# Attention and two feed-forward layers on one core: score matmuls of two heads side by side, norms by matmul, and an offset for every kind of task

## The chip, the core and the metric

One core of a Trainium2 chip runs the whole program. The metric is the device time of one execution in microseconds (us); three runs of the kernel before took 1132.02 to 1135.79 us, median 1133.86.

## What is computed

```python
# attention: batch 4, 8 heads, 576 positions, 64 dimensions per head
scores = (q @ k.T) / sqrt(64)
x = log1p(|i - j|) / log1p(max(i, 1))
scores += relu(x * w1 + b1) @ w2          # 32 hidden units, one bias per head
a = softmax(scores) @ v                   # -> 2304 tokens x 512
# first feed-forward layer (512 -> 2048 -> 512), then the second
h = relu(a @ moe_w_in);  y = (s * h*h + b) @ moe_w_out
g = y @ moe2_w_in;       out = (g - tanh(g)) @ moe2_w_out
```

## The kernel before

Every matmul operand is split into a high part in fp16 and a low part (the rest, also fp16), each under one scale that is a power of two; a product is the sum of high x high, high x low and low x high. The scales come from norms, which are computed on the chip first.

**Units.** Attention is cut into 144 units: one head of one batch entry with 128 rows of queries (128 "full" units), or two heads with the last 64 rows (16 "half" units). Batch entries 0 and 1 come first (72 units), then 2 and 3. A unit's work, in `unit_tasks` (line 716):

- `qk` on TensorE (L749): scores into a PSUM tile `sp`. In the array's 128 rows lie 64 dimensions of the keys' high part and 64 of their low part, and the queries stand there twice, so that a unit takes four matmuls of 288 columns (two halves of the 576 keys, the queries' high and low part). A half unit puts its two heads into 64 columns each and takes eight.
- `ttr` on VectorE (L763, L767): adds the bias `bi`, takes the row's maximum.
- `ex` on ScalarE (L773): the exponential into `e`, with the row's sum. `hi` (L782 on VectorE or L784 on ScalarE) copies `e` to fp16, `lo` (L790, GpSimd) takes the rest, `tr` (L796, a DMA) transposes both into `et`.
- `pv` on TensorE (L809, L816): 14 matmuls with the values into `xp`.

`x_tasks` scales a group of four units, splits it and transposes it into `xt`, the input of the first feed-forward layer. Two `sp` tiles, two `e`, three `hl`, four `et` and one `xp` exist.

**Before the units.** `scan_tasks` loads keys, queries and values of a batch entry and sums their squares on ScalarE (L591); `part_sum` (L423) adds over partitions, `qk_scales` makes the scales. `k_tasks` makes high and low part of two heads' keys in four steps of 64 partitions each (L359/L357 for the high part, L362 for the low), `q_tasks` those of a group's queries, after a DMA from `qd`, where the queries stand twice. `bias_tasks` makes the biases of 16 rows for all heads, 36 times: hidden units (L454, L458 or L462), 8 matmuls (L466, tile `pb`), a copy to `et` and a DMA to DRAM. `norm_in_tasks`, `w1_conv`, `w1_split` prepare the weights of the first layer (L918 to L924, L974, L362); `cols_out` (L1134, tile `pcs`) sums columns of its second matrix once all of that is split, and `out_done` (L1028, `bcol`) follows.

**The feed-forward layers.** The first runs in nine blocks of 256 tokens, each as soon as its units are done: 192 matmuls `ph` (L1221), relu and square on ScalarE, high part on VectorE, low part on GpSimd, 192 matmuls `po` (L1289). When all units are done (`turn`) the weights of the second layer are loaded and split where the attention's tiles were. Its matmuls are `pg` (L1517) and `pq` (L1564).

**The order.** Nothing is ordered by hand. Every step is a task with a list of engines and costs, tasks that it needs, buffers that it takes, and a due time `prio`. `Schedule.forward` plays the program with these costs: again and again it takes the engine that can start first, and on it, among the tasks that can start within `EPS` of that, the one due first. The order in which it does so is the order of the instructions on each engine, fixed in the program. `tau(u)` gives the due time of unit u; bias, keys, queries and blocks hang on it by constants (lines 26 to 31).

## Time and profile before

| | us |
|---|---|
| median of three runs (lowest, highest) | 1133.86 (1132.02, 1135.79) |
| profiled execution: time | 1135.39 |
| profiled execution: span | 1133.6 |
| TensorE matmul busy | 1026.7 |
| VectorE busy | 786.0 |
| ScalarE busy | 569.0 |
| GpSimd busy | 344.5 |

The span runs from the first to the last instruction; 1.8 us of the execution lie around it. Busy times are sums over an engine's instructions. Matmuls are pipelined and their ends are modelled, so what one matmul really takes is read from the distance of starts, not from its own duration. The granted clock is the share of TensorE's full 2.4 GHz that the chip let through.

### The profile page before, as it was taken

The page shows a single profiled execution, that of the slowest core. Times are in us where ns is not written, and L with a number is a line of the kernel's source. Part 1 is how long each engine was busy: PE and PEld are TensorE (multiplying, and loading weights), DVE is VectorE, ACT ScalarE, POOL GpSimd, SP SyncE. Part 2 cuts the span into 40 slices and gives each one's busy share as a digit, 9 for nine tenths or more (in the row PEclk, how much of TensorE's full clock was granted, in tenths as well). Part 3 has the DMA queues.
Part 4 walks back from the last instruction along what each step waited for, and adds up shares of the span by engine and source line. Part 5 has one row for each costly group of instructions (what it writes and reads, how often), then busy time and mean ns, then how long its engine had stood idle before and what let it go on. Part 6 is the DMA issues. An engine that isn't in the chain of part 4 may idle for free.

```text
span 1133.6 us, 23200 instructions
## 1 busy us (share of the span) xinstructions
PE 1026.7 (91%) x9023; PEld 695.8 (61%) x9026; DVE 786.0 (69%) x1642; ACT 569.0 (50%) x1116; POOL 344.5 (30%) x371
## 2 busy tenths in 40 slices
PE   3366787998999989999999999989999999999998
PEld 1132364776787777878888788877554444444443
DVE  6999899988657898786875668898655444354310
ACT  6999887667667585565663444641211111111100
POOL 6043154436545266575764321400000000000000
PEclk9566797899999999999999999999999999999999
DMA  9887885888999989999997453441010000000000
GB/s 336 288 213 213 200 277 118 186 191 203 197 216 244 237 191 182 195 176 191 199 187 129 161 179 126 154 130 43 5 46 10 19 10 10 19 10 15 14 19 28
DMA packets 260701, 157.79 MB, mean 139 GB/s; under 512 B 199408, under 2 KB 226672, under 8 KB 260592
## 3 DMA queue, kind: packets, MB, share of 16 engines
q1 hardware_dynamic: 260592, 156.33, 58.2%
q8 instruction: 70, 1.15, 0.4%
q14 instruction: 39, 0.32, 0.1%
HBM read 89.04 MB, written 20.05 MB: 96 GB/s over the span
## 4 chain that ended last, share of the span: by engine, by line
PE 60%; DVE 20%; DMA 7%; ACT 5%; issue 4%; POOL 2%; SPq 1%; DVEq 0%; ACTq 0%; POOLq 0%
PE pq L1564 16%; PE pg L1517 16%; PE po L1289 10%; PE ph L1221 8%; DMA et<-hl 5%; PE sp L749 3%; PE pb L466 3%; DVE sp L763 2%; PE xp L809 2%; DVE ks L362 1%; PE xp L816 1%; DVE w1big L921 1%; ACT e L773 1%; DVE vp L362 1%; DVE hr L1244 1%
## 5 line engine op out<-in xcount | busy, mean ns | idle before, releaser
L790 POOL TENSOR_TENSOR hl<-e,hl 128x64 f16<-128x64 f32 (+1 forms) x288 | 232.2, 829 | 229.9 <-ACT hl L784 82.9
L1289 PE MATMUL po<-hr,w1big 128*128 128x256 f16 x1728 | 204.6, 273 | 6.9 <-ACT x L1308 4.3
L1564 PE MATMUL pq<-w1big,w2big 128*128 128x512 f16 (+1 forms) x960 | 195.3, 358 | 0.0
L1289 PEld LDWEIGHTS <-w1big 128*128 128x128 f16 x1728 | 165.8, 98 | 33.6 <-issue 8.3
L1221 PEld LDWEIGHTS <-w1big 128*128 128x128 f16 x1728 | 166.9, 98 | 31.1 <-issue 10.1
L1525 ACT ACTIVATE t<-pg,ich 128x512 f32<-128x512 f32 (+1 forms) x80 | 51.5, 644 | 245.6 <-PE pg L1517 245.6
L1517 PE MATMUL pg<-hr,w2big 128*128 128x512 f16 x768 | 173.6, 379 | 0.0
L1529 DVE SCALAR_TENSOR_TENSOR t<-pg,ich,t 128x512 f32<-128x512 f32 (+1 forms) x80 | 55.7, 696 | 148.9 <-ACT t L1525 148.9
L1517 PEld LDWEIGHTS <-w2big 128*128 128x128 f16 x960 | 95.0, 99 | 96.7 <-issue 4.7
L1564 PEld LDWEIGHTS <-w2big 128*128 128x128 f16 x960 | 93.9, 98 | 94.0
L773 ACT ACTIVATE e<-sp,mx 128x576 f32<-128x576 f32 x144 | 105.6, 733 | 76.0 <-POOL hl L790 48.6
L1248 POOL TENSOR_TENSOR hr<-r,hr 128x512 f16<-128x512 f32 x72 | 96.6, 1342 | 153.8 <-DVE hr L1244 137.0
L763 DVE CUSTOM_DVE_ANT_0 sp<-sp,bi 128x576 f32<-128x576 f32 x144 | 109.3, 759 | 41.5 <-PE sp L749 21.1
L749 PE MATMUL sp<-ks,qs 128*128 128x288 f16 (+1 forms) x640 | 101.7, 303 | 22.2 <-ACT e L773 20.0
L1221 PE MATMUL ph<-xt_own,w1big 128*128 128x256 f16 x960 | 113.8, 274 | 4.4 <-ACT et L359 2.6
L1221 PE MATMUL ph<-w1big 128*128 128x256 f16 x768 | 88.2, 273 | 0.3 <-DVE na L1180 0.3
L749 PEld LDWEIGHTS <-qs 128*128 128x128 f16 (+1 forms) x640 | 54.3, 104 | 47.6 <-issue 31.8
L809 PEld LDWEIGHTS <-et 128*128 128x128 f16 (+1 forms) x1440 | 57.0, 103 | 28.5 <-issue 13.2
L809 PE MATMUL xp<-vp,et 128*128 128x64 f16 (+1 forms) x1440 | 65.2, 198 | 9.9 <-DMA et<-hl 6.1
L784 ACT ACTIVATE hl<-e 128x576 f16<-128x576 f32 x92 | 62.0, 677 | 16.4 <-DMA et<-hl 15.0
L466 PE MATMUL pb<-hr,cst_sb 128*32 128x288 f32 x268 | 41.2, 589 | 28.4 <-DVE et L357 10.9
L1234 ACT ACTIVATE r<-ph 128x512 f32<-128x512 f32 x72 | 42.6, 591 | 40.2 <-PE ph L1221 38.5
(165 smaller groups left out, 1286.2 us busy)
## 6 DMA issues: line engine op xcount, KB each, us to landing
bi<-btd SPq DMA_DIRECT2D x64, 288.0 KB, 3.7
btd<-et SPq DMA_DIRECT2D x36, 288.0 KB, 4.3
qst<-in_qd SPq DMA_DIRECT2D x36, 256.0 KB, 3.8
w1big<-in_win SPq DMA_DIRECT2D x8, 1024.0 KB, 7.9
w1big<-in_wout SPq DMA_DIRECT2D x8, 1024.0 KB, 6.5
w2raw<-in_win SPq DMA_DIRECT2D x8, 1024.0 KB, 5.5
w2raw<-in_wout SPq DMA_DIRECT2D x8, 1024.0 KB, 4.9
x2d<-x SPq DMA_DIRECT2D x36, 128.0 KB, 3.0
```

The source lines that it names most:

```text
L466: nc.tensor.matmul(out=pb[32 * t:32 * t + 32, 0:HS], lhsT=w2d_sb, rhs=hid_t[Q, t][:, hf * HS:(hf + 1) * HS], start=True, stop=True,)
L749: nc.tensor.matmul(out=s_[r0:r0 + r, hf, 0:HS], lhsT=qs.tile[:, s, c * r:c * r + r], rhs=ks.tile[:, a, hf * HS:(hf + 1) * HS], start=s == ...
L763: nc.vector.tensor_tensor_reduce(out=st, in0=st, in1=bi.tile.rearrange("p (a b) -> p a b", a=2), scale=-1.0 / KAP, scalar=3.0e38, op0=ALU. ...
L773: nc.scalar.activation(out=put(e, row_tile("e")).rearrange("p (a b) -> p a b", a=2), in_=sp.tile[:, :, 0:HS], func=AF.Exp, scale=-1.0, bia ...
L784: nc.scalar.activation(out=h[:, 0:S], in_=e.tile, func=AF.Copy)
L790: nc.gpsimd.tensor_tensor(out=hl.tile[:, o:o + m], in0=e.tile[:, c:c + m], in1=hl.tile[:, c:c + m], op=ALU.subtract)
L809: nc.tensor.matmul(out=xp[r0:r0 + r, col:col + 64], lhsT=et.tile[:, n, r0:r0 + r], rhs=vp.tile[:, 0, n % 5, 64 * a:64 * a + 64], start=n = ...
L1221: nc.tensor.matmul(out=ph.tile[:, fi, :], lhsT=win_ap(1, sw, m, f), rhs=xa(sx, m), start=m == 0 and j == 0, stop=m == KM - 1 and j == 2,)
L1248: nc.gpsimd.tensor_tensor(out=rh[:, :, 1, :], in0=r.tile, in1=rh[:, :, 0, :], op=ALU.subtract)
L1289: nc.tensor.matmul(out=po.tile[:, :NB1], lhsT=wout_ap(1, sw, f, c), rhs=rhl[f // 8][:, f % 8, sr, :], start=f == 0 and j == 0, stop=f == K ...
L1517: nc.tensor.matmul(out=pg.tile[:, :n], lhsT=win_ap(2, sw, m, f), rhs=xh[:, sx, m, :n], start=m == 0 and i == 0, stop=m == KM - 1 and i == 2,)
L1564: nc.tensor.matmul(out=pq.tile[:, :n], lhsT=wout_ap(2, sw, f, c), rhs=g[:, sr, :n], start=f == 0 and i == 0, stop=f == KF - 1 and i == 2,)
```

## The change

1. **Scores (`qk`).** Keys of two heads lie in the array's rows 0 to 63 and 64 to 127, their high and low part in two tiles. The two heads of a pair of full units are done by one task of 12 matmuls of 64 rows each, which alternate between the halves of the array and write into two `sp` tiles; it takes both. A half unit takes 12 as well. The order of units inside a batch entry changes with it (`unit_of`): two heads of a pair follow each other.
2. **Keys and queries.** `k_tasks` has two steps of 128 partitions in place of four of 64. `q_tasks` loads all eight heads of a batch entry and 128 rows once, from `qT`, in place of two loads from `qd`: 20 loads, copies and low parts in place of 36.
3. **First norms.** For batch entries 0 and 1 the squares on ScalarE are replaced by matmuls (tile `gram`, 112 of 128 columns) of the upper 16 bits of each value with themselves, and a maximum over each row on VectorE.
4. **Order.** Costs of the player are changed (GpSimd's bias tile 2.45 for 1.5, `PACE`, `HOP`, `COLD`), due constants too, and a table `SHIFT` adds an offset to the due time of each kind of task, some 500 of them. A ring's check counts all buffers that a task takes.
5. **Transposes of `x`.** The layout of `xt` follows the new order of heads; a half group takes four small transposes in place of two.

```diff
-SHARE0, QP, QA, SCU, QG = 31, 8, 19, 48, 7
-T0, R0, T1, RU = 58.44, 2.06, 98.62, 3.64
+SHARE0, QP, QA, SCU, QG = 21, 8, 19, 15, 7
+T0, R0, T1, RU = 56.98, 2.21, 35.64, 3.33
...
-EPS, COLD = 0.02, 100.0
+EPS, COLD, COLD_PACE = 0.02, 190.0, 1.45
+SHIFT = {
+    ".begin": 7.58, ".fn": -21.6, ".lambda": 12.08, "scan0.fn": -26.47, "scan0.mm": -51.47, "scan0.add": -45.69,
...
-    HOP = 0.2
+    HOP = 0.23
+    PACE = dict(pe=1.0, act=1.02, dve=1.06, pool=1.0)
...
-        t.opts, t.fn, t.prio, t.takes = opts, fn, prio, tuple(takes)
+        t.key = self.tag + "." + fn.__code__.co_name.strip("<>")
+        t.opts, t.fn, t.prio, t.takes = opts, fn, prio + SHIFT.get(t.key, 0.0), tuple(takes)
...
+    def unit_of(u):
+
+        b, it, g, k = units[u]
+        if rows_of[it] < 128:
+            return b, it, k, None, k
+        return b, it, 2 * g + k // 2, k % 2, 2 * (k % 2) + k // 2
...
-                {DVE: 0.45, ACT: 0.67, **({POOL: 1.5} if Q < QG else {})}, lambda e, Q=Q, t=t: hid(Q, t, e), deps, d, [hid_i[Q, t]] if Q >= QA else []
+                {DVE: 0.45, ACT: 0.67, **({POOL: 2.45} if Q < QG else {})}, lambda e, Q=Q, t=t: hid(Q, t, e), deps, d, [hid_i[Q, t]] if Q >= QA else []
...
-            ts = sc.add({ACT: 0.16 + 0.86e-3 * n_}, sq, [tl, t0], prio, [jk] if jk else [], [st] if st else [])
...
+                for c in range(n_ // 128):
+                    x = t[:, c, :, 1]
+                    nc.tensor.matmul(
+                        out=gi.tile[:, int(kq), :], lhsT=x, rhs=x, start=c == 0 and col in (0, 4, 8),
+                        stop=c == n_ // 128 - 1 and col in (1, 5, 10),
+                    )
+            tg = sc.add({PE: 0.07 * n_ / 128 + 0.1}, mm, [tl, gram[1]], prio - 500, [gi] if new else [], [gi])
...
+                    nc.vector.tensor_reduce(out=s3, in_=gi.tile[:, 0:n, :], op=ALU.max, axis=AX.X)
...
-        h0 = sc.add({ACT: 0.79, DVE: 0.46}, lambda e: hi(0, e), deps, due - 4, [ks], us)
-        h1 = sc.add({ACT: 0.79, DVE: 0.46}, lambda e: hi(1, e), deps + [h0], due - 4, [], [ks] + us)
-        l0 = sc.add({DVE: 0.86}, lambda e: lo(0, e), [h0], due - 2, [], [ks] + us)
-        l1 = sc.add({DVE: 0.86}, lambda e: lo(1, e), [h1], due - 2, [], [ks] + us)
+        th = sc.add({ACT: 0.67, DVE: 0.46}, hi, deps, due - 4, [ks], us)
+        tl = sc.add(
+            {DVE: 0.78}, lambda _: low_part(ks.tile[:, 1], src(), sc_t[b]["k"], ks.tile[:, 0]), [th], due - 2, [],
+            [ks] + us,
+        )
...
+        src = qT[b, :, it * 128:it * 128 + r].rearrange("(p k) r -> k p r", k=128)
...
-            s_ = put(sp, ps_s.tile([128, 2, 512], F32, tag="s", name="sp"))
+
             r = rows_of[it]
-            heads = [(0, g, p)] if full else [(0, 0, 2 * p), (64, 1, 2 * p + 1)]
-            for s in range(2):
-                for hf in range(2):
-                    for r0, a, c in heads:
+            to = [s_of[v] for v in ((u - 1, u) if full else (u,))]
+            for i in to:
+                put(i, ps_s.tile([128, 2, 512], F32, tag="s", name="sp"))
+            for hf in range(2):
+                for n, (sq, sk) in enumerate(((0, 0), (0, 1), (1, 0))):
+                    for h in range(2):
+                        half = hf if full or h == 0 else 1 - hf
+                        out = to[h].tile[:, half, 0:HS] if full else to[0].tile[64 * h:64 * h + 64, half, 0:HS]
                         nc.tensor.matmul(
-                            out=s_[r0:r0 + r, hf, 0:HS], lhsT=qs.tile[:, s, c * r:c * r + r],
-                            rhs=ks.tile[:, a, hf * HS:(hf + 1) * HS], start=s == 0, stop=s == 1,
+                            out=out, lhsT=qs.tile[64 * h:64 * h + 64, sq, p * r:p * r + r],
+                            rhs=ks.tile[64 * h:64 * h + 64, sk, half * HS:(half + 1) * HS], start=n == 0, stop=n == 2,
                         )
...
+        if not full or a == 1:
+            two = [s_of[u - 1], sp] if full else [sp]
+            t_qkm[u] = sc.add(
+                {PE: 0.95}, qk, t_klo[b, p] + t_khi[b, p] + [t_qlo[b, it], t_last[0]] + first, d - 1000, two, [ks, qs],
+            )
```

How the order moves is shown at three places. The first is the start of ScalarE, where the norms were (`e,ss` are the squares, `hr` and `xt_own` hidden units of the bias, `et` their evacuation, `ks` the keys' high part). Before:

```order
L462 ACT_TABLE_LOAD
L462 ACTIVATE hr<-u_sb,cst_sb 128x576 x2
L591 ACTIVATE e,ss_124<-w1big 128x1152 x2
L462 ACTIVATE hr<-u_sb,cst_sb 128x576
L359 ACTIVATE et<-pb,cst_sb 128x576
L591 ACTIVATE e,ss_124<-w1big 128x1152
L462 ACTIVATE hr<-u_sb,cst_sb 128x576 x4
L591 ACTIVATE e,ss_124<-w1big 128x1152
L462 ACTIVATE hr<-u_sb,cst_sb 128x576 x2
L359 ACTIVATE ks<-w1big,qkc_303 64x576
```

And the changed kernel there:

```order
L556 ACT_TABLE_LOAD
L556 ACTIVATE hr<-u_sb,cst_sb 128x576 x2
L556 ACTIVATE xt_own<-u_sb,cst_sb 128x576
L444 ACTIVATE et<-pb,cst_sb 128x576
L556 ACTIVATE xt_own<-u_sb,cst_sb 128x576
L556 ACTIVATE hr<-u_sb,cst_sb 128x576 x2
L444 ACTIVATE et<-pb,cst_sb 128x576
L556 ACTIVATE xt_own<-u_sb,cst_sb 128x576
L444 ACTIVATE et<-pb,cst_sb 128x576
L556 ACTIVATE hr<-u_sb,cst_sb 128x576 x3
L444 ACTIVATE ks<-w1big,qkc_314 128x576 x3
```

The squares are gone, bias work has their place, and the keys come as rows of 128 partitions.

The second is VectorE where the first layer's second matrix is ready (`w1big<-w1big,w1o_c` are its last splits, `bcol` follows the column sums; `ISA sp,mx` is a unit's score row). Before:

```order
L362 SCALAR_TENSOR_TENSOR w1big<-w1big,w1o_c 128x1024 x2
L763 ISA sp,mx<-sp,bi 128x2x288
L763 ISA mx 128x1
L767 TENSOR_SCALAR mx<-mx 128x1
L763 ISA sp,mx<-sp,bi 128x2x288
L763 ISA mx 128x1
L767 TENSOR_SCALAR mx<-mx 128x1
L869 CAST xh<-xf 128x256
L870 TENSOR_TENSOR xh<-xf,xh 128x256
L362 SCALAR_TENSOR_TENSOR qs<-qst,qkc_398,qs 128x512
L458 TENSOR_SCALAR hid<-u_sb,cst_sb 128x576 x3
L1028 TENSOR_SCALAR bcol<-pcs,w1o_ic,cst_sb 128x4
```

And the changed kernel there:

```order
L447 SCALAR_TENSOR_TENSOR w1big<-w1big,w1o_c 128x1024
L447 SCALAR_TENSOR_TENSOR qs<-qst,qkc_314,qs 128x512
L1009 CAST xh<-xf 128x256
L1010 TENSOR_TENSOR xh<-xf,xh 128x256
L901 ISA sp,mx<-sp,bi 128x2x288
L901 ISA mx 128x1
L905 TENSOR_SCALAR mx<-mx 128x1
L901 ISA sp,mx<-sp,bi 128x2x288
L901 ISA mx 128x1
L905 TENSOR_SCALAR mx<-mx 128x1
L1388 CAST hr<-r 128x2x256
L1172 TENSOR_SCALAR bcol<-pcs,w1o_ic,cst_sb 128x4
```

Ahead of `bcol` stand 27 score rows before and 30 now. On TensorE, ahead of the column sums, stand 192 bias matmuls, the scores of 27 units and the values of 24 before; 232, 30 and 28 now; and all 192 `ph` of the first block in both.

The third is TensorE at one unit's scores, in batch entries 2 and 3. Before:

```order
L816 MATMUL xp_6577<-vp_6068,et_6569 128x64
L749 LDWEIGHTS qs_6603
L749 MATMUL sp_6717<-ks_5679,qs_6603 128x288
L749 LDWEIGHTS qs_6603
L749 MATMUL sp_6717<-ks_5679,qs_6603 128x288
```

And the changed kernel, the first third of a pair's scores:

```order
L955 MATMUL xp_6930<-vp_5359,et_6828 128x64
L869 LDWEIGHTS qs_6809
L869 MATMUL sp_6950<-ks_5773,qs_6809 128x288
L869 LDWEIGHTS qs_6809
L869 MATMUL sp_6951<-ks_5773,qs_6809 128x288
```

The matmuls now alternate between two score tiles; a pair has twelve, where two units had eight.

## Rows read from the trace of the kernel before

**Rows 1.** The page's busy times and its 40 slices of the span.

```profile
PE 1026.7 (91%) x9023; PEld 695.8 (61%) x9026; DVE 786.0 (69%) x1642; ACT 569.0 (50%) x1116; POOL 344.5 (30%) x371
...
PE   3366787998999989999999999989999999999998
...
DVE  6999899988657898786875668898655444354310
...
PEclk9566797899999999999999999999999999999999
```

**Rows 2.** Busy time of each engine in four stretches.

```profile
core 0: us, PE busy (x) PEld busy (x) DVE busy (x) ACT busy (x) POOL busy (x), PEclk, DMA share, GB/s
0.00:204.00 204.00, 130.52 (x1192) 71.96 (x1196) 184.89 (x340) 171.92 (x295) 78.66 (x73) 0.75 0.81 231
204.00:620.00 416.00, 396.12 (x4760) 324.48 (x4759) 318.60 (x834) 264.59 (x579) 232.10 (x276) 0.99 1.00 198
620.00:770.00 150.00, 140.61 (x1286) 124.18 (x1285) 119.53 (x185) 72.80 (x152) 33.72 (x24) 0.98 0.43 142
770.00:1133.60 363.60, 359.47 (x1791) 175.16 (x1789) 162.95 (x284) 59.70 (x90) 0.00 (x0) 1.00 0.06 19
```

**Rows 3.** Timeline of TensorE at the column sums (start, us, what, idle before).

```profile
198.58 3.57 PE L1134 MATMUL pcs<-onesh,w1big 128*128 128x1 f16 x128
```

**Rows 4.** Timeline of VectorE at the same place.

```profile
195.33 2.97 DVE L362 SCALAR_TENSOR_TENSOR w1big<-w1big,w1o_c 128x1024 f16<-128x1024 f32 x2
...
203.63 0.27 DVE L1028 TENSOR_SCALAR bcol<-pcs,w1o_ic,cst_sb 128x4 f32<-128x4 f32 x1
```

**Rows 5.** Groups by line and shape: count, busy us, mean ns, idle before.

```profile
L362 DVE SCALAR_TENSOR_TENSOR ks<-w1big,qkc,ks 64x576 f16<-64x576 f32 x16 | 13.0, 814 | 0.4
...
L362 DVE SCALAR_TENSOR_TENSOR qs<-qst,qkc,qs 128x512 f16<-128x512 f32 x36 | 32.7, 907 | 0.4
...
L591 ACT ACTIVATE e<-w1big 128x1152 bf16<-128x1152 f32 x8 | 9.2, 1156 | 1.0 <-DMA w1big<-in_kT 0.8 <-DMA w1big<-in_qT 0.2
...
L454 POOL TENSOR_SCALAR hr<-u_sb,cst_sb 128x576 f32<-128x576 f32 x6 | 14.7, 2462 | 5.3 <-DVE u_sb L431 5.3
```

**Rows 6.** Timeline of TensorE, full units at 518 us, half units at 601 us.

```profile
518.00 0.43 PE L809 MATMUL xp<-vp,et 128*128 128x64 f16 x9
518.26 0.41 PE L816 MATMUL xp<-vp,et 128*128 128x64 f16 x5
518.61 0.66 PE L749 MATMUL sp<-ks,qs 128*128 128x288 f16 x4
519.11 1.47 PE L1289 MATMUL po<-hr,w1big 128*128 128x256 f16 x12
520.42 0.65 PE L749 MATMUL sp<-ks,qs 128*128 128x288 f16 x4
...
601.32 0.68 PE L749 MATMUL sp<-ks,qs 128*64 128x288 f16 x8
601.93 1.48 PE L1289 MATMUL po<-hr,w1big 128*128 128x256 f16 x12
```

**Rows 7.** TensorE's bias matmuls at the start: timeline, and the group in 0 to 100 us.

```profile
6.27 1.42 PE L466 MATMUL pb<-hr,cst_sb 128*32 128x288 f32 x4 [6.27 <-DVE hr L458]
...
13.02 1.18 PE L466 MATMUL pb<-hr,cst_sb 128*32 128x288 f32 x16
...
L466 PE MATMUL pb<-hr,cst_sb 128*32 128x288 f32 x176 | 26.5, 575 | 22.0 <-DVE et L357 10.9 <-DVE hr L458 6.3 <-POOL hr L454 4.2
```

**Rows 8.** Timeline of all engines: the unit whose scores start at 518.61.

```profile
519.84 0.76 DVE L763 CUSTOM_DVE_ANT_0 sp<-sp,bi 128x576 f32<-128x576 f32 x1
...
520.69 0.15 DVE L767 TENSOR_SCALAR mx<-mx 128x1 f32<-128x1 f32 x1
...
522.81 0.74 ACT L773 ACTIVATE e<-sp,mx 128x576 f32<-128x576 f32 x1 [1.15 <-POOL hl L790]
523.45 0.19 ACT L773 ACTIVATION_READ_ACCUMULATOR e<-sp,mx 128x1 f32 x1
```

**Rows 9.** The page's group of score matmuls, with what ended the idle time before them.

```profile
L749 PE MATMUL sp<-ks,qs 128*128 128x288 f16 (+1 forms) x640 | 101.7, 303 | 22.2 <-ACT e L773 20.0
```

More of the change, by code (lines that the diff above doesn't have):

```diff
@@ L53 @@
     __slots__ = (
-        "opts", "fn", "deps", "prio", "takes", "eng", "at", "end", "done", "left", "next", "seq",
+        "opts", "fn", "deps", "prio", "takes", "eng", "at", "end", "done", "left", "next", "seq", "key",
     )
+ENGINES = ("pe", "act", "dve", "pool", "sp", "turn")
 class Schedule:
-    HOP = 0.2
+    HOP = 0.23
+    PACE = dict(pe=1.0, act=1.02, dve=1.06, pool=1.0)
     DMA_START, DMA_DONE = 0.65, 2.0
@@ L147, in forward @@
             else:
-                if eng == "pe" and at < COLD:
-                    cost = cost * 1.6
+                cost *= COLD_PACE if eng == "pe" and at < COLD else self.PACE.get(eng, 0.0)
                 free[eng] = t.end = at + cost
@@ L375, in tile_kernel @@
                 groups += [(b, it, g) for g in range(2) for b in pr]
-    units = [g + (p,) for g in groups for p in range(NP)]
+    units = [g + (k,) for g in groups for k in range(NP)]
     NG, NU = len(groups), len(units)
@@ L384, in tau, with units_of @@
         return T0 + R0 * u if u < 16 else T1 + RU * (u - 16)
+    def unit_of(u):
[3 more added lines that the diff above has]
+        return b, it, 2 * g + k // 2, k % 2, 2 * (k % 2) + k // 2
+    def units_of(**kw):
+        for u in range(NU):
+            b, it, p, a, c = unit_of(u)
+            d = dict(b=b, it=it, p=p)
+            if all(d[k] == v for k, v in kw.items()):
+                yield u
     def first_unit(**kw):
-        for u, (b, it, g, p) in enumerate(units):
-            d = dict(b=b, it=it, g=g, p=p)
-            if all(d[k] == v for k, v in kw.items()):
-                return u
+        return next(units_of(**kw))
     def last_unit(**kw):
-        return max(
-            u for u, (b, it, g, p) in enumerate(units) if all(dict(b=b, it=it, g=g, p=p)[k] == v for k, v in kw.items())
-        )
+        return max(units_of(**kw))
     ones16 = const.tile([128, 128], BF16, name="ones16")
@@ new lines, in qk @@
+                            rhs=ks.tile[64 * h:64 * h + 64, sk, half * HS:(half + 1) * HS], start=n == 0, stop=n == 2,
+                        )
+        first = [x for Q in range(QP) for x in t_bmm[Q]] if u < 2 else []
+        if not full or a == 1:
[3 more added lines that the diff above has]
+            )
+            t_last[0] = t_qkm[u]
+            if full:
+                t_qkm[u - 1] = t_qkm[u]
+                unit_rest(u - 1)
+            unit_rest(u)
@@ L758, in unit_tasks, with unit_rest @@
+    s_of, t_last = {}, [None]
+    def unit_rest(u):
+        sc.tag = f"u{u // 4 if u < 40 else 10 + u // 16}"
+        b, it, p, a, col = unit_of(u)
+        n, k = u // NP, u % NP
+        full = rows_of[it] == 128
+        d = tau(u)
+        bi, sp = bi_of[u], s_of[u]
+        e, hl, et = inst("e"), inst("hl"), inst("et")
+        vp, sm_i, xp_i = vp_t[b, p], sum_of[n], xp_of[n]
         mx = {}
```

188 lines of the change are left out of this document (105 added, 83 removed), and 75 rows, old and new, of the table SHIFT.

## Prediction

> **What bounds the kernel now.** I read the page's slices first, then the busy time by stretch, then timelines where the bound changes. In the slices [rows 1] TensorE is starved for the first seven of 40 and its granted clock stays below full speed there, while VectorE is at 8 or 9 tenths; afterwards TensorE is nearly always full. The stretches [rows 2] put numbers on it. Up to 204 us VectorE is busy 184.9 us of 204, ScalarE 171.9, TensorE 130.5 at a granted clock of 0.75. From 204 to 620 TensorE is busy 396.1 of 416 at 0.99 and VectorE 318.6; from 620 to 770 it is 140.6 of 150, and after that 359.5 of 363.6. So there are two laws. Before 204 us VectorE and ScalarE set the pace; after it, what TensorE has still to do sets the end, and work taken from the other engines buys nothing there.
>
> The border is one event. The first layer's second matmuls wait for the column sums, which start at 198.58 [rows 3] right after VectorE's last two splits, from 195.33 on; its first use of the sums is at 203.63 [rows 4]. The question is therefore: when does this event come, and how much TensorE work is left behind it?
>
> **The change, part by part.**
>
> *VectorE up to the event.* The order gives the counts. Eight low parts of keys fewer (0.81 each) and three of queries (0.91) [rows 5] are 9.2 us less. But three score rows more, five bias tiles more and two weight copies more stand ahead of the event, each between 0.5 and 1.1 us, together about 9 us. VectorE's work up to the event stays 185 us: the change does not bring it nearer, it puts more units and more bias ahead of it.
>
> *ScalarE up to the event.* Twelve squares of some 1.1 us [rows 5] and two small ones go, about 17 us with the reads of their sums; bias tiles and evacuations fill a good part. ScalarE was not the fuller engine, so I count nothing. Without that cover, VectorE's work, the 17 us would be an upper bound of the gain.
>
> *TensorE up to the event.* 40 bias matmuls more: 16 take 1.18 at full clock [rows 7], so 3.0 us. Scores of three more units: 0.50 each, from 518.61 to 519.11. Values of four more: 0.61 each, from 518.00 to 518.61 [rows 6]. Together 3.0 + 1.5 + 2.4 = 6.9 us that are not left behind the event. The 112 norm matmuls lie where TensorE has 74 us of idle time. They stand in the queue ahead of the first bias matmuls, which started at 6.27 [rows 7]; these now wait for the first keys to land. Before, bias matmuls lost 4.2 us to GpSimd's late tiles [rows 7], which took 2.46 each [rows 5] where the old cost was 1.5; with 2.45 the order no longer holds a queue behind them. I take 3 us gain for these two together, between a loss of 2.8 (the first bias at 9 us, where the second tile came anyway) and a gain of 4.2, nearer to the gain because the long wait of 10.9 us for an evacuation [rows 7] lies behind the same tiles.
>
> *Scores after the event.* 49 pairs and 16 half units are left. A slot of 288 columns is 0.50 / 4 = 0.125. Half units show what two matmuls in different halves of the array's columns cost: eight start at 601.32 and the next work at 601.93 [rows 6], 0.61 for four slots, so they run two at a time, with 0.11 on top of 0.50. No row shows two halves of the rows. Bounds: six slots with nothing on top, 0.75 a pair; twelve slots one after the other and 0.11, 1.61. I take six and 0.11, 0.86, from the half unit's row, which is nearest: 0.14 less than two units, times 49 is 6.9 us less. A half unit has six slots where it had four: 0.25 more, times 16 is 4.0 more. Net 2.9 less. The 0.11 speaks against the change, as every pair now pays what only half units paid. The Trainium skill's page "TensorEngine Tiling (Array Packing)", section "Key Properties", says the same in general: changing the tiling mode drains TensorE. A reader who took the row for an accident of half units would write 0.75 and 12 us for 6.9; by that rule the 0.11 stays.
>
> *The rest.* 16 loads of queries fewer, eight transposes more, VectorE's and ScalarE's savings after 204: nothing, as TensorE's work covers them; transposes that came late would cost what rival B and C say. The order behind the last unit holds the same blocks (2.84 left before, 2.88 now), so the tail stays.
>
> *Sum*, against the profiled execution (1135.4; 1.5 above the median): -6.9 - 3.0 - 2.9 = -12.8, that is 1122.6, and **1121** as a median.
>
> **The rivals.**
>
> *B, the front really shrinks.* VectorE stands idle for 19.1 us up to 204, TensorE for 19.9 us from 204 to 620 [rows 2]. The new offsets and costs may take half of each: 6.5 us more than my 3, and 10: 1104. For it: VectorE is lighter by 17 or so instructions after the event, so score rows come sooner. Against it: the order must fit the chip, and the old one left such gaps as well.
>
> *C, a pair holds both score tiles* (the other side). Now a unit's scores are made while the other unit's are read; score matmuls lost 20 us in all waiting for exponentials [rows 9]. A pair takes both tiles, and the next pair waits for its second exponential. One unit's chain was 5.0 us: scores at 518.61 [rows 6], score row at 519.84, exponential at 522.81 after 1.15 of waiting for GpSimd, sum read at 523.64 [rows 8]. The pair adds 0.36 on TensorE and a second score row (0.76, plus its read and its offset, 1.05): 6.4. The order leaves 6.2 us of TensorE work from one pair's scores to the next, on average. It decides from there: with half of the 1.15 for the second exponential it is 6.8, a stall of 0.6 at 49 pairs, 29 us: 1150. Against it: VectorE and ScalarE have more room, and not every unit waits for GpSimd.
>
> *D, the two halves of the rows do not run together.* Then a pair is 1.61, 0.61 more than now, times 49 is 30, and a half unit 1.61 for 0.61, 16 more: 46 in place of -2.9, 1170. Against it: halves of the columns do run together [rows 6].
>
> *E, they overlap in part, or the order gives back what it gains.* If a slot takes 0.163 for 0.125, a pair is 1.09 and a half unit too: +4.4 and +7.7, in place of -2.9: 1136. The Trainium skill's page "TensorE: Matmul & The Clock Gate", section "Part 3: Packing small matmuls", measured 3.07 times for four row tiles, not 4; 0.125 x 4 / 3.07 is an estimate of a slot by that page, 0.163. Here the traces speak for the full overlap, of columns only.
>
> **How the numbers follow.** My case 0.44, B 0.18, C 0.16, D 0.08, E 0.14. No change means within 0.3%, 3.4 us, about what a measurement can tell here. Faster: my case but for 0.01, B, and 0.03 of E, 0.64. The same: 0.11, nearly all from E. Slower: C, D and a little of E, 0.25. The range goes from 1096 (B with three quarters of the idle time) to 1150 (C); outside are D and the far ends of B and C, under 0.2. My case alone would be 1110 to 1130.
>
> **What would show it.** Column sums still near 199 us, with 30 units scored; 12 score matmuls of a pair in about 0.86 where the clock is full; TensorE filled over 95% from there to 620; VectorE's busy time down by 40 or 50 us without effect after 204. I am wrong if a pair takes over 1.0, if score matmuls wait for exponentials much more than 20 us, or if the column sums come before 190 or after 210.

## The result, and the profile after

Against the kernel before on the same chip the change took 1120.5 us (median of four, 1118.59 to 1123.4) where that took 1132.99: ratio 0.9888, 95% interval 0.9857 to 0.9919. That is faster by 1.1%, clear of what a measurement can tell. Predicted were 1121, with 1096 to 1150 as the range. The profiled executions lie 16.2 us apart (1135.39 and 1119.2), more than the medians, because the one of before was above its median and the one of after below.

The page's busy times and slices of the changed kernel, for [rows 1]:

```profile
PE 1027.3 (92%) x9458; PEld 688.3 (62%) x9458; DVE 751.0 (67%) x1567; ACT 557.4 (50%) x1098; POOL 347.8 (31%) x370
...
PE   5657678999999899999998999999999999999998
...
DVE  6999999966678577777663669999738237212530
...
PEclk9667798899999899999998999999999999999999
```

TensorE's digits in the first seven slices have risen, VectorE has lost 35 us, and behind the front the picture is the old one. By stretch, for [rows 2] (the last stretch is 16 us shorter):

```profile
core 0: us, PE busy (x) PEld busy (x) DVE busy (x) ACT busy (x) POOL busy (x), PEclk, DMA share, GB/s
0.00:204.00 204.00, 142.90 (x1518) 78.79 (x1520) 187.20 (x352) 167.39 (x292) 88.62 (x76) 0.80 0.85 239
204.00:620.00 416.00, 397.69 (x4996) 321.36 (x4993) 287.23 (x771) 260.33 (x569) 226.06 (x276) 0.98 0.90 187
620.00:770.00 150.00, 143.42 (x1298) 126.51 (x1296) 129.03 (x201) 73.29 (x155) 33.08 (x20) 1.00 0.39 132
770.00:1117.40 347.40, 343.25 (x1654) 161.69 (x1652) 147.57 (x246) 56.38 (x83) 0.00 (x0) 1.00 0.06 20
```

Up to 204 us TensorE does 12.4 us more, at a granted clock of 0.80 for 0.75, while VectorE is as full as before. From 204 to 620 VectorE is 31 us lighter and TensorE is as busy as it was: the saving there went nowhere, since VectorE was not what TensorE waited for.

TensorE's timeline at three places: the column sums [rows 3], a pair's scores [rows 6], and the last values of attention (start, us, what, idle before):

```profile
197.16 0.67 PE L1278 MATMUL pcs<-onesh,w1big 128*128 128x1 f16 x21
198.11 2.92 PE L1278 MATMUL pcs<-onesh,w1big 128*128 128x1 f16 x107 [0.28 <-DVE w1big L447]
...
496.06 0.43 PE L948 MATMUL xp<-vp,et 128*128 128x64 f16 x9 [1.32 <-DMA et<-hl]
496.33 0.41 PE L955 MATMUL xp<-vp,et 128*128 128x64 f16 x5
496.55 0.93 PE L869 MATMUL sp<-ks,qs 64*128 64x288 f16 x12
497.41 2.79 PE L1434 MATMUL po<-hr,w1big 128*128 128x256 f16 x24
...
606.69 0.69 PE L948 MATMUL xp<-vp,et 128*64 128x64 f16 x18 [3.55 <-DMA et<-hl]
607.19 0.60 PE L955 MATMUL xp<-vp,et 128*64 128x64 f16 x10
607.72 6.38 PE L1365 MATMUL ph<-w1big 128*128 128x256 f16 x36
```

The event, as the start of the column sums is called here, came at 197.16 (198.58 before). A pair takes 0.86 here, and 0.84 in the median of 41 pairs between 260 and 620 us. The last stop of 3.55 us is new; before, the longest wait of that kind behind the sums was 1.1. The page's groups of score and value matmuls, for [rows 9]:

```profile
L869 PE MATMUL sp<-ks,qs 64*128 64x288 f16 (+1 forms) x960 | 84.0, 302 | 12.9 <-ACT e L911 10.3
...
L948 PE MATMUL xp<-vp,et 128*128 128x64 f16 (+1 forms) x1440 | 65.4, 198 | 17.0 <-DMA et<-hl 11.5
```

The group of values before:

```profile
L809 PE MATMUL xp<-vp,et 128*128 128x64 f16 (+1 forms) x1440 | 65.2, 198 | 9.9 <-DMA et<-hl 6.1
```

Waits of scores for exponentials fell from 20.0 to 10.3 us; waits of values for transposes rose from 6.1 to 11.5.

**The ledger.** The span fell by 16.2: 1.4 because the column sums came sooner, 14.8 because less lay behind them (920.2 us to the end for 935.0). Read from the distance of TensorE's starts behind the sums, bias matmuls took 5.3 less, scores 6.1, values 3.5, the second layer 2.2, and idle time fell by 4.0; the first layer's matmuls took 6.3 more.

By counts and prices, as the prediction adds up, the 14.8 are made up otherwise: work moved ahead of the sums 9.8 (80 records of bias matmuls by 1.18 / 16 [rows 7], 5.9; scores and values as predicted, 1.5 and 2.4); scores 3.8 (49 pairs at 0.842 for 1.00, 7.7 less; 16 half units at 0.855 for 0.61, 3.9 more); waits 3.8 (the releasers behind the sums add up to 28.5 us before, 24.7 after). That is 17.4, so some 2.6 went back. Two things are there for it. The granted clock fell in two stretches after the new waits (380 to 400 us at 0.83, 603 to 618 at 0.77). And a first-layer matmul right ahead of a pair's scores takes 0.205 to the next start, where it took 0.109 ahead of a full unit's scores before; 34 pairs behind the sums stand there, 3.3 us, which the 0.842 does not hold (see the last section).

The waits fell mainly at one place. Between the last work of the first layer and the bulk of the second's, TensorE waited 4.54 us in the kernel before, and the granted clock was 0.76 after it (TensorE's timeline, and a stretch):

```profile
766.19 2.08 PE L1517 MATMUL pg<-xt_own,w2big 128*128 128x256 f16 x9 [4.54 <-DVE t L1529]
...
766.00:776.00 10.00, 9.81 (x70) 7.83 (x70) 8.68 (x23) 2.37 (x5) 0.00 (x0) 0.76 0.01 2
```

In the change these matmuls wait 0.3 us for VectorE:

```profile
PE pg L1666 <- DVE hr L447: 0.3, 1, 0.3
```

### The profile page after: what moved, and what is told of

It reads as the page before. It is cut to its first block, busy times and chain, and to the rows that moved or that the text cites. A ratio compares the mean times of both kernels' runs of the same rounds, so it can differ in the third digit from the quotient of the medians.

```text
span 1117.4 us, 23943 instructions
## 1 busy us (share of the span) xinstructions
PE 1027.3 (92%) x9458; PEld 688.3 (62%) x9458; DVE 751.0 (67%) x1567; ACT 557.4 (50%) x1098; POOL 347.8 (31%) x370
## 4 chain that ended last, share of the span: by engine, by line
PE 61%; DVE 10%; ACT 4%; DMA 4%; issue 3%; SPq 2%; POOL 1%; POOLq 0%; DVEq 0%; ACTq 0%
PE pg L1666 16%; PE pq L1714 16%; PE po L1434 11%; PE ph L1365 10%; PE sp L869 3%; DMA et<-hl 3%; PE xp L948 2%; DVE sp L901 2%; PE xp L955 2%; ACT e L911 1%; DVE w1big L447 1%; DVE hr L1388 1%; POOL hl L929 1%; SPq L1027 1%; ACT r L1378 1%
## 5 line engine op out<-in xcount | busy, mean ns | idle before, releaser
L929 POOL TENSOR_TENSOR hl<-e,hl 128x64 f16<-128x64 f32 (+1 forms) x288 | 235.2, 839 | 217.4 <-ACT hl L923 121.1
L1714 PE MATMUL pq<-w1big,w2big 128*128 128x512 f16 (+1 forms) x960 | 189.7, 358 | 0.0
L1666 PE MATMUL pg<-hr,w2big 128*128 128x512 f16 x768 | 168.0, 379 | 0.3 <-DVE hr L447 0.3
L869 PE MATMUL sp<-ks,qs 64*128 64x288 f16 (+1 forms) x960 | 84.0, 302 | 12.9 <-ACT e L911 10.3
L1365 PE MATMUL ph<-w1big 128*128 128x256 f16 x768 | 92.2, 280 | 1.5 <-ACT r L1378 1.5
L923 ACT ACTIVATE hl<-e 128x576 f16<-128x576 f32 x109 | 74.0, 680 | 14.2 <-DMA et<-hl 10.4
L948 PE MATMUL xp<-vp,et 128*128 128x64 f16 (+1 forms) x1440 | 65.4, 198 | 17.0 <-DMA et<-hl 11.5
L948 PEld LDWEIGHTS <-et 128*128 128x128 f16 (+1 forms) x1440 | 54.2, 103 | 42.7 <-issue 23.5
L1726 ACT ACTIVATE o<-pq,osc 128x512 f32<-128x512 f32 (+1 forms) x20 | 12.9, 644 | 132.6 <-PE pq L1714 132.6
L869 PEld LDWEIGHTS <-qs 64*128 64x128 f16 (+1 forms) x960 | 47.3, 100 | 37.6 <-issue 26.1
L1388 DVE CAST hr<-r 128x512 f16<-128x512 f32 x72 | 43.6, 606 | 33.8 <-ACT r L1383 28.8
```

The costliest lines, as they stand in the source:

```text
L869: nc.tensor.matmul(out=out, lhsT=qs.tile[64 * h:64 * h + 64, sq, p * r:p * r + r], rhs=ks.tile[64 * h:64 * h + 64, sk, half * HS:(half + 1 ...
L923: nc.scalar.activation(out=h[:, 0:S], in_=e.tile, func=AF.Copy)
L929: nc.gpsimd.tensor_tensor(out=hl.tile[:, o:o + m], in0=e.tile[:, c:c + m], in1=hl.tile[:, c:c + m], op=ALU.subtract)
L948: nc.tensor.matmul(out=xp[r0:r0 + r, o:o + 64], lhsT=et.tile[:, n, r0:r0 + r], rhs=vp.tile[:, 0, n % 5, 64 * h:64 * h + 64], start=n == 0, ...
L1365: nc.tensor.matmul(out=ph.tile[:, fi, :], lhsT=win_ap(1, sw, m, f), rhs=xa(sx, m), start=m == 0 and j == 0, stop=m == KM - 1 and j == 2,)
L1666: nc.tensor.matmul(out=pg.tile[:, :n], lhsT=win_ap(2, sw, m, f), rhs=xh[:, sx, m, :n], start=m == 0 and i == 0, stop=m == KM - 1 and i == 2,)
```

## Experiments

All were compared with the kernel before on their own chip, 1134.44, 1134.03 and 1135.01 us in the three sets; the change itself stands at ratio 0.9888.

### Do two halves of the rows run together?

**e1: one head after the other.**

```diff
-            for hf in range(2):
-                for n, (sq, sk) in enumerate(((0, 0), (0, 1), (1, 0))):
-                    for h in range(2):
+            for h in range(2):
+                for hf in range(2):
+                    for n, (sq, sk) in enumerate(((0, 0), (0, 1), (1, 0))):
```

> The changed kernel (1120.5 us), with the twelve score matmuls of a pair issued head by head in place of alternately, so that two matmuls in a row use the same half of the array; everything else, the order included, is the same. Theory (two halves of the rows run at a time, and TensorE's work counts only behind the column sums at 198 us): a pair goes from 0.84 to twelve slots of 0.1225 and 0.11, 1.58; 49 pairs and 16 half units behind the sums pay 0.73 each, 48 us: 1168, and the column sums still start near 198. Rival 1 (the halves never ran together): no difference. Rival 2 (TensorE's work counts from the start): 15 pairs more pay, 59 us, 1179.

Measured 1124.73 (1123.43 to 1127.44), ratio 0.9912 (0.9885 to 0.9939). The expectation was far off: a pair takes 1.10, not 1.58. Timeline of TensorE in e1:

```profile
501.13 1.16 PE L869 MATMUL sp<-ks,qs 64*128 64x288 f16 x12
502.22 1.05 PE L1434 MATMUL po<-hr,w1big 128*128 128x256 f16 x8
```

The single records of this pair show how. There are two series at a spacing of 0.123, each beginning with a matmul that waits for its score tile: one starts at 0, 0.12, 0.25, 0.37, 0.49 and 0.61 us, the other at 0.25, 0.39, 0.51, 0.63, 0.76 and 0.88. The second head's first matmul started with the first head's third and so went past three matmuls that stand ahead of it in the program. The column sums did not move (196.7). By count 0.26 on 65 visits is 17 us, and by the distance of starts 16.2 more were spent on scores behind the sums. Much of it came back: the profiled span is only 5.8 us longer than the change's. Idle time behind the sums fell by 5.6 (score waits for exponentials, 2.6 us in the change, are below 0.5 here, and the last values waited 2.94 us for 3.55), and the first layer's matmuls took 3.8 less; after that last wait the clock stayed at 1.00 where the change has 0.77.

**e9: all twelve in the same half.**

```diff
+                        g = 0 if full else 64 * h
-                            out=out, lhsT=qs.tile[64 * h:64 * h + 64, sq, p * r:p * r + r],
-                            rhs=ks.tile[64 * h:64 * h + 64, sk, half * HS:(half + 1) * HS], ...
+                            out=out, lhsT=qs.tile[g:g + 64, sq, p * r:p * r + r],
+                            rhs=ks.tile[g:g + 64, sk, half * HS:(half + 1) * HS], ...
```

> All twelve score matmuls of a full pair use rows 0 to 63 of the array (the odd head's scores are computed from the even head's keys and queries, so that part of the output is not the reference's); the order and the count of instructions stay. It prices what head by head did not: twelve slots with no other half to run in. Theory (halves of the rows run two at a time, and head by head still overlapped from the fourth matmul on, because the next head's first one started as the third of the first head did): nothing can overlap now, a pair takes 12 x 0.1225 + 0.11 = 1.58 where the clock is full, 0.74 more than 0.84; at 49 pairs behind the column sums that is 36 us, less what it takes out of waits there: 1120.5 + 30 to 36 = 1150 to 1156. Rival (score matmuls of one half overlap among themselves as well, and 1.10 was simply their rate): a pair stays at 1.10, 1124 to 1126.

Measured 1148.62 (1144.65 to 1151.9), ratio 1.0124 (1.0081 to 1.0168). Timeline of TensorE in e9:

```profile
505.18 1.64 PE L870 MATMUL sp<-ks,qs 64*128 64x288 f16 x12
506.75 0.44 PE L949 MATMUL xp<-vp,et 128*128 128x64 f16 x9
```

A pair takes 1.57, the expected 1.58 to 0.01 (rival D of the prediction has 1.61). The time is 28 us above the change where 30 to 36 were expected; the last values came 29.6 later (636.3 for 606.7). By the distance of starts the scores behind the sums took 34.8 us more and the sums came 2.5 later, while 6.8 of idle time were taken back.

**e10: runs of three.** The loops in the order column half, head, product.

```diff
-                for n, (sq, sk) in enumerate(((0, 0), (0, 1), (1, 0))):
-                    for h in range(2):
+                for h in range(2):
+                    for n, (sq, sk) in enumerate(((0, 0), (0, 1), (1, 0))):
```

> The score matmuls of a pair are issued in runs of three of one head (three of head 0, three of head 1, three, three), the rest as in the change. Theory (a half of the rows takes the matmuls that wait for it off the queue, up to three behind the one that runs; head by head, six in a run, the other head's first one started together with the third): runs of three leave no half empty but at the ends, a pair takes 0.84 to 0.90, and the time is the change's, 1119 to 1123. Rival (TensorE looks only at its queue's head, two at a time only where neighbours lie in different halves): only the borders of the runs overlap, a pair takes about 12 slots less 3, 1.21, and with 65 visits at 0.37 more, of which head by head gave back half, the time is 1129 to 1140.

Measured 1121.15 (1118.84 to 1126.56), ratio 0.9886 (0.9856 to 0.9916). Timeline of TensorE in e10:

```profile
503.28 0.92 PE L869 MATMUL sp<-ks,qs 64*128 64x288 f16 x12
504.12 1.48 PE L1434 MATMUL po<-hr,w1big 128*128 128x256 f16 x12
```

A pair takes 0.84 here (0.848 in the median), as in the change. Strict alternation is not needed; runs of three fill both halves, runs of six do not.

### What sets the column sums?

**e3 and e4: the keys' low parts in two steps of 64 partitions**, for batch entries 0 and 1 (e3) or 2 and 3 (e4: `b >= 2`).

```diff
+        def low_steps():
+            for r in ((slice(0, 64), slice(64, 128)) if b < 2 else (slice(0, 128),)):
+                low_part(ks.tile[r, 1], src()[r], sc_t[b]["k"][r], ks.tile[r, 0])
-            {DVE: 0.78}, lambda _: low_part(ks.tile[:, 1], src(), sc_t[b]["k"], ks.tile[:, 0]), ...
+            {DVE: 0.78}, lambda _: low_steps(), ...
```

> The changed kernel, with the low parts of the keys of batch entries 0 and 1 made in two steps of 64 partitions again, 8 VectorE instructions of 0.81 us more, all ahead of the column sums; the order of everything else is the same. Theory (VectorE paces the front): 6.5 us longer, 1127, with the column sums at 204 to 205. Rival (the front is paced by ScalarE, GpSimd or waits): under 2 us.

> The same 8 instructions more, but for the keys of batch entries 2 and 3, at 330 to 410 us, where TensorE is the bound. Theory: nothing, within 1.5 us of 1120.5. Rival (VectorE paces there as well, through the score rows): 5 to 7 us longer.

e3 took 1126.0 (1123.48 to 1127.36), ratio 0.9916 (0.9892 to 0.994); the first scores came 6.1 us later (56.0), the column sums 6.6 (203.7). e4 took 1122.36 (1118.58 to 1125.51), ratio 0.9885 (0.986 to 0.9911): no difference, sums at 196.6. The same eight instructions on VectorE cost 3 us (by the ratios) to 5.5 (by the medians) ahead of the event and nothing behind it.

**e5: ScalarE's squares put back.**

```diff
+            jk = inst("e")
+            def sq_too(_):
+                o = put(jk, row_tile("e")).bitcast(BF16)[:rows, :n_]
+                nc.scalar.activation(out=o, in_=where[:rows], func=AF.Square, accum_out=ss[:rows, col:col + 1])
+            gram[2].append(sc.add({ACT: 0.0}, sq_too, [tl, t0], prio, [jk]))
...
```

> The fourteen squares of the first two batches' keys and queries stand on ScalarE again, beside the matmuls that now make the norms (their sums go nowhere); TensorE's order is the change's. 12 of 1.1 us and two small ones with the reads of their sums: 17 us more on ScalarE ahead of the column sums. Theory (VectorE's work sets when the column sums come, ScalarE has some 30 us to spare there): column sums at 197 to 200, time within 3 us of the change's, 1118 to 1124. Rival (taking ScalarE's squares away is what keeps the front in time): column sums 8 to 17 us later, 1128 to 1137.

Measured 1123.46 (1120.58 to 1125.26), ratio 0.9897 (0.9868 to 0.9927). Between the two: the sums came at 201.4, 4.2 later, not 17 and not 0. The first scores were 3.9 later (53.8). VectorE waited ahead of the sums for two things of ScalarE for which it did not wait in the change:

```profile
DVE vp L447 <- ACT vp L444: 2.2, 1, 2.2
...
DVE ks L447 <- ACT ks L444: 1.7, 1, 1.7
```

That is 3.9 of the 4.2, so the delay is ScalarE's, passed on through VectorE.

**VectorE's time up to the sums.** Its busy time from 0 to the start of the sums, and the rest of that time, in six kernels (us):

| | column sums | VectorE busy | VectorE idle |
|---|---|---|---|
| before | 198.58 | 179.61 | 19.0 |
| change | 197.16 | 180.50 | 16.7 |
| e3 | 203.72 | 187.65 | 16.1 |
| e5 | 201.39 | 180.79 | 20.6 |
| e7 (below) | 205.44 | 187.32 | 18.1 |
| e2 (below) | 212.42 | 182.94 | 29.5 |

Each is read against the kernel that it was made from: e7 from the kernel before, the others from the change. In e3 and e7 the event comes later by VectorE's added work, in e5 and e2 mainly by VectorE's added idle time.

### What is the order worth?

**e2: no offsets** (`SHIFT = {}`).

> The changed kernel with an empty table of offsets; all other parts stay, the player makes another order. Its order has 36 units scored ahead of the column sums where the change has 30, and some 5 us more of VectorE work ahead of them. Theory (the end follows from when the sums come and what TensorE has left then): sums 5 us later, 6 us less TensorE work behind them, so within 5 us of the change, 1116 to 1126: the offsets are not the gain. Rival (the offsets are the gain): back at 1130 or more, with TensorE idle behind 204 us grown by 10 us or more.

Measured 1131.84 (1128.19 to 1136.16), ratio 0.9978 (0.9959 to 0.9997). Expected was that most of the gain would stay; the rival holds. The sums (timeline of TensorE in e2):

```profile
212.42 3.58 PE L1201 MATMUL pcs<-onesh,w1big 128*128 128x1 f16 x128
```

Waits of scores for exponentials ahead of them (us in total, times, longest), in e2:

```profile
PE sp L792 <- ACT e L834: 21.9, 17, 3.5
```

and in the change:

```profile
PE sp L869 <- ACT e L911: 7.7, 9, 1.9
```

Without the table the player starts scoring 6.8 us sooner and has 36 units ahead of the sums where the change has 30, but the scores then wait 14 us more for exponentials, and the sums come 15.3 later. For VectorE that is 2.4 us of work and 12.8 of idle time. Behind the sums e2 takes 915.6 us to the end for 920.2, only 4.6 less: by the distance of starts the scores and values of the six units are 9.2 less, but idle time is 6.9 more, and the wait at the start of the second layer is back (6.1). 15.3 - 4.6 = 10.7 is the difference of the spans.

**e11: offsets of the front alone.** Of the table's 441 offsets the 174 stay that name tasks of the front (`EARLY` lists them: biases, first scans, keys, values and queries, first-layer weights, its first block, units 0 to 31).

```diff
+SHIFT = {k: v for k, v in SHIFT.items() if k[0] == "." or k.split(".")[0].rstrip("01234" if k[:4] == "bias" else "") in EARLY}
```

> Of the table of offsets only the 174 stay that belong to the kinds of task of the front (biases, the first two batches' scans, keys and values, the first queries, the first layer's weights and its first block, units 0 to 31); the other 267, for everything behind, go. TensorE's order stays the change's up to the column sums (21 units of bias rows aside: 180 score matmuls, 392 value matmuls and 232 bias matmuls stand ahead of them in both). Theory (without the table the column sums came 15 us later while what TensorE did behind them took as long, 915.6 against 920.2 us to the end; so the table's gain is the front's): column sums at 196 to 199, time within 3 us of the change's, 1118 to 1124. Rival (the offsets behind the front keep TensorE fed there): column sums the same, but 5 to 10 us more behind them, 1126 to 1131.

Measured 1122.7 (1119.92 to 1126.29), ratio 0.989 (0.9862 to 0.9919); sums at 196.8. The other 267 offsets are worth nothing that can be measured in the time. The trace does show one thing that they do: without them the wait at the start of the second layer is there, in e11 as in e2.

```profile
PE pg L1668 <- DVE t L1680: 6.1, 1, 6.1
```

Behind the sums e11 takes 924.7 us to the end for 920.2.

**e7 and e8: one cost.** GpSimd's bias tile at 2.45 in the kernel before, at 1.5 in the change.

```diff
-                {DVE: 0.45, ACT: 0.67, **({POOL: 1.5} if Q < QG else {})}, ...
+                {DVE: 0.45, ACT: 0.67, **({POOL: 2.45} if Q < QG else {})}, ...
```

> The kernel before with one number of the change: a hidden tile of the first bias blocks is planned with 2.45 us on GpSimd, not 1.5. Theory (my third term: an order that knows how long GpSimd takes holds no queue behind a tile that is not there yet; 3 us with the first bias matmuls' later start): bias matmuls wait less than 2 us for GpSimd where they waited 4.2, column sums 2 to 5 us sooner, 1128 to 1131. Rival (the bias waits lie where TensorE idles anyway, and the plan only moves them): column sums within 2 us of 198.6, time within 3 us of 1134.

> The change with one number taken back: a hidden tile of the first bias blocks planned with 1.5 us on GpSimd. The plan then comes out otherwise at the front (20 units ahead of the column sums where there were 30, and the first block's 192 matmuls behind them). Theory (table and costs are one fit, and a single number moved in it spoils the order at the front, as it did in the kernel before): 5 to 20 us more than the change, 1126 to 1140. Rival (the table holds by itself, what stands ahead of the sums is taken back behind them at no loss): within 3 us of the change, 1118 to 1124.

e7 took 1138.67 (1136.15 to 1142.23), ratio 1.0041 (1.0024 to 1.0057): slower, which neither theory had. Waits of TensorE ahead of 204 us in e7, and the same two before:

```profile
PE sp L749 <- ACT e L773: 26.7, 17, 8.2
...
PE pb L466 <- POOL hr L454: 1.1, 3, 0.5
```

```profile
PE sp L749 <- ACT e L773: 12.5, 11, 3.4
...
PE pb L466 <- POOL hr L454: 4.2, 4, 1.2
```

The wait that the cost was to remove fell by 3.1 us; another grew by 14.2, and the sums came at 205.4. The new cost gave a new order: the scores of 32 units stand ahead of the sums where 27 stood, VectorE has 7.7 us more work up to them, and they come 6.9 later; behind them 929.3 us are left for 935.0. So e7 prices the cost together with the order that the player makes of it, not the cost by itself. e8 took 1147.53 (1145.66 to 1148.46), ratio 1.0107 (1.0074 to 1.014), 27 us above the change, where at most 20 were expected. Its column sums came at 170.6, 26.6 sooner than the change's, and it ended 29 later: the plan put them ahead of the first block's 192 matmuls and of ten units that the change has ahead of them, and 976.0 us lay behind them for 920.2. Of these 55.8 more, by the distance of starts, 19.9 are the block's `ph`, 11.7 scores and values, 3.1 bias matmuls and 17.6 idle time.

### The new wait at the end of attention

SP's queue in the change (start, us, what):

```profile
590.48 6.18 SPq L935 DMA_TRANSPOSE et<-hl  x3
596.70 5.96 SPq L1027 DMA_TRANSPOSE xt_own<-xh  x4
602.76 0.52 SPq L300 DMA_DIRECT2D x2d<-x  x1
603.45 1.30 SPq L935 DMA_TRANSPOSE et<-hl  x1
```

The four small transposes of a half row's output (two before) take 5.96 us of SP's queue (1.23, 1.17, 1.24 and 2.12); the player counts 0.62 for each (`{SP: (0.62, 0.83 if full else 0.21)}`, where the second number is the transfer). The last unit's weights were ready at 596.93, when GpSimd had made their low part, and stood behind the four.

**e13: the last unit's transpose first.**

```diff
+    hold, tr_last = t_xtr[len(groups) - 2][0], t_tr[len(units) - 1]
+    hold.deps.append(tr_last)
+    hold.left += 1
+    tr_last.next.append(hold)
     sc.run()
```

> One more dependency in the plan: the four small transposes of the last row but one's output (L1027) wait in SP's order for the last unit's transpose of its weights (L935). Nothing else moves: TensorE, VectorE, ScalarE and GpSimd keep the change's order. In the change that last transpose stood behind the four on SP (596.70 to 602.66) and was issued at 603.45, though its input was there at 596.9; TensorE waited 3.55 us for it from 603.14 on, and its clock fell to 0.76 after that (36 matmuls from 607.72 took 6.2 us to the next work for 4.0 elsewhere). Theory (behind the column sums every us that TensorE waits is at the end, and the clock it loses too): the wait goes and the clock stays up, 4 to 6 us less, 1114.5 to 1116.5. Rival (the wait only moves: the four transposes are late then, and TensorE waits for the last block's input): 1119 to 1122.

Measured 1114.33 (1113.28 to 1118.48), ratio 0.9823 (0.9795 to 0.9851). This version beats both kernels. SP's queue in e13:

```profile
596.85 1.31 SPq L935 DMA_TRANSPOSE et<-hl  x1
598.20 12.89 SPq L1027 DMA_TRANSPOSE xt_own<-xh  x8
```

Timeline of TensorE in e13:

```profile
602.88 0.47 PE L948 MATMUL xp<-vp,et 128*64 128x64 f16 x18
603.18 0.44 PE L955 MATMUL xp<-vp,et 128*64 128x64 f16 x10
603.56 4.10 PE L1365 MATMUL ph<-w1big 128*128 128x256 f16 x36
```

The granted clock from 603 to 618 us, in the change:

```profile
603.00:618.00 15.00, 11.45 (x104) 9.28 (x103) 4.36 (x14) 4.47 (x8) 2.70 (x3) 0.77 0.36 95
```

and in e13:

```profile
603.00:618.00 15.00, 15.00 (x161) 13.41 (x160) 6.29 (x17) 7.82 (x14) 5.77 (x5) 1.00 0.43 148
```

The wait of 3.55 is gone, and with it 2.3 that the 36 matmuls behind it took longer (6.21 to the next work in the change, 3.94 here): after the stop the clock was granted at a mean of 0.77, part of the stretch at the lower of its two levels, 1.2 GHz; without the stop it was 2.4 throughout. Behind the sums e13 takes 915.0 us to the end for 920.2.

**e14: a second hold.** The same for the other half row: its transposes wait for the load of the next queries, on top of e13's hold.

```diff
+    for hold, first in ((t_xtr[16][0], t_ql[groups[19][:2]]), (t_xtr[NG - 2][0], t_tr[NU - 1])):
+        hold.deps.append(first)
+        hold.left += 1
+        first.next.append(hold)
     sc.run()
```

> The same hold, and a second one of the same kind: the four small transposes of the first half row's output wait for the load of the next queries (both heads rows of the second half of the batch), which in the change were issued behind them at 376.8; scores waited 1.84 and 0.37 us for those queries at 381, values 2.02 for a transpose and the next block 1.55, and the clock was 0.76 from 380 to 394. The plan moves here from unit 74 or so on, on all engines. Theory (as above): up to 6 us of waits and some 3 of clock less than with the first hold alone, 1106 to 1112. Rival (SP's queue is full there, 6 us of transposes merely stand ahead of other loads): within 3 us of the first hold alone or slower, 1113 to 1120.

Measured 1114.78 (1109.44 to 1116.8), ratio 0.9805 (0.9773 to 0.9837): not to be told from e13. The order of all engines moves behind unit 74 here, so e14 does not price its hold alone. The waits at 381 us went, and one came at 405 (timelines of TensorE and of SP in e14):

```profile
405.02 0.66 PE L948 MATMUL xp<-vp,et 128*128 128x64 f16 x9 [8.48 <-DMA et<-hl]
```

```profile
380.84 11.87 SPq L1027 DMA_TRANSPOSE xt_own<-xh  x8
392.81 0.52 SPq L300 DMA_DIRECT2D x2d<-x  x1
...
398.06 5.93 SPq L935 DMA_TRANSPOSE et<-hl  x2
```

The time fits the rival: in the middle of attention eight small transposes, now in one piece, merely stand ahead of something else on SP's queue.

## Why the prediction was right, and which terms were not

- **The event.** "Column sums still near 199 us, with 30 units scored": 197.16 (198.58 before), with 30. Right, and for the reason given: VectorE's work up to the event hardly changed (180.5 us for 179.6). The 1.4 by which the event came sooner is VectorE's idle time, 2.3 less, minus 0.9 more of work. The law behind it, that work on VectorE counts ahead of the event and not behind it, is shown by e3 and e4. Behind it VectorE became 31 us lighter between 204 and 620, where the prediction named 40 or 50 as the sign, and as it said without effect.
- **ScalarE counted at nothing.** Too low: e5 puts up to 4.2 us of the event on the squares, some 1 to 3 us in the time. The prediction's bound of 17 was far off the other way.
- **6.9 us of work moved ahead.** One term was mis-sized. The order counts 40 bias matmuls more ahead of the sums; the trace records each of them twice (464 ahead for 384), and the price of 1.18 for 16 is one of records. It is 80 x 1.18 / 16 = 5.9 where the prediction had 3.0 (5.3 by the distance of starts), and the work moved is 9.8.
- **3.0 us for the first bias and GpSimd's cost.** This step failed. It counted waits of TensorE ahead of the event as a gain, though by the prediction's own law VectorE sets the event. The bias matmuls' wait for GpSimd did go (0.2 us for 4.2), but TensorE waited there for the first keys instead (11.2 for the norm matmuls, 8.8 of it at the very start, where the first bias matmuls stood at 6.27), and all that the front gained is the 1.4. Put into the kernel before, the new cost and the order that follows from it make it 4.6 us slower (e7).
- **Scores 2.9 us less.** By count it is 3.8, as a pair was predicted at 0.86 and is 0.84. The step that carried it, two halves of the rows run together as two of the columns do, is shown by e9 against the change: 1.57 and 0.84 with the same count of matmuls.
- **The drain.** The 0.11 that the prediction kept on top of six slots is there: six of 0.1225 are 0.735, and a pair takes 0.842. The Trainium skill's page "TensorEngine Tiling (Array Packing)", section "Key Properties", says that changing the tiling mode drains TensorE; the trace agrees, with about 0.1 us at each change. What the prediction missed is that a visit of scores changes the mode twice, on the way in and on the way out. The way in is paid by the first-layer matmul ahead (34 pairs, 3.3 us), except behind values, where it is free (below).
- **Partial overlap (E).** Nothing of it: a slot is 0.1225, where 1.09 a pair would need 0.163. The speedup of 3.07 by four row tiles on the Trainium skill's page "TensorE: Matmul & The Clock Gate", section "Part 3: Packing small matmuls — row/col tiling", is not what two tiles of 64 rows do here: 1.57 to 0.84 is 1.87 with the 0.11 and 2 without it.
- **Rival C** (the pair holds both score tiles). Its sign did not come: these waits fell behind the sums from 7.6 to 2.6 us. In the front of e2 they are 21.9 us. But in e7, where a unit holds one tile as in the kernel before, they are 26.7, so no run shows that holding both tiles is what costs in e2. What e2 and e11 do show is that the gain hangs on the offsets of the front, which the prediction did not name: without the table the whole rest of the change is worth 0.2% (e2).
- **The rest at nothing.** Wrong at two places that nearly cancel. The "eight transposes more" were counted at nothing: they stood ahead of the last unit's transpose on SP and cost some 6 us in time, wait and clock, as e13 shows. It also has "so the tail stays": the wait of 4.5 us at the start of the second layer went, and the second layer's matmuls took 2.2 less.
- **The sum.** Between the profiled executions the change gained 16.2 where the sum had 12.8; between the medians, 12.5. That 1121 lies half a microsecond from 1120.5 is luck: the bias term was 2.9 too small, the front 1.6 too large, and the changes of mode, the transposes and the start of the second layer were not in it. The mechanism, one event set by VectorE and the TensorE work left behind it, is what the runs bear out.

What stays open: whether the waits at 381 us can be had back by another order of SP's queue (e14 only moved them), and what the many idle stretches of VectorE in e2's front have in common.

## What to carry to other kernels

Price a change to a kernel with one bound before an event and another after it by two numbers, when the event comes and how much is left behind it: e8 had its event 27 us sooner and ended 29 later. The event comes after the work of the engine that sets it plus that engine's idle time: e3 moved the one, e2 the other. A planner's costs and offsets are one fit: the truer cost for GpSimd made the kernel before slower, and taking it back made the change slower by 27 us. Count transfers on their queue by number as well as by size, and look for what stands behind a moved step there: a small transpose took as long as one of nine times its size. And price a new shape of matmul with its neighbours, as part of its cost may stand in theirs.

## What the runs showed of the hardware

- Score matmuls of one half of the rows overtake those of the other. In e1 the second head's first one started with the first head's third, ahead of three that precede it in the program; runs of three cost nothing (0.84), runs of six 0.26 a pair. The Trainium skill's page "TensorE: Matmul & The Clock Gate", section "Part 3: Packing small matmuls — row/col tiling", says that matmuls start and end in program order; for tiles in different rows these traces show otherwise, and the measurement decides.
- A change between matmuls of 128 rows and of 64 costs about 0.1 us each way. Behind the sums a first-layer matmul takes 0.109 to the next start, and 0.205 when a pair's scores come next (34 cases); ahead of a full unit's scores before it took 0.109 (28 cases). On the way out a pair's last score takes 0.215 to the next start, where a slot is 0.1225. The fourteenth value matmul of a unit has 64 rows itself: it starts 0.126 after the thirteenth, where the others start 0.029 apart, and a pair's scores start 0.007 after it (10 cases). Scores of 128 rows in the kernel before started 0.132 after it (49 cases), and half units' scores, which use 64 rows and 64 columns, 0.130 (4 cases). So the fourteen take 0.48 to 0.49 ahead of a pair (0.49 in the rows above, 496.06 to 496.55) and 0.61 ahead of the scores of before [rows 6].
- A transpose of 128 x 2 x 64 takes 1.16 to 1.25 us of SP's queue in most cases (three of the four at 596.70, the fourth 2.12), as much as one of 128 x 9 x 128 (1.30 at 603.45), nine times its size.
